# A new written-out order for a one-core attention and feed-forward kernel, with some products moved between two engines

## The chip, the core and the metric

The kernel runs on one core of a Trainium2 chip. The metric is device microseconds of one execution. The kernel before took 254.58 us, the median of three runs (254.56 to 255.01).

## The reference

The computation is linear attention with polynomial sketches, followed by a multiplicative feed-forward block (FFN). In NumPy, cut to what matters:

```python
batch, n_heads, seq, head_dim, r = 4, 4, 1088, 32, 8          # q, k, v: (4, 4, 1088, 32) float32
def phi(x):                                                   # S1, S2: (8, 32) float64
    a = einsum('rd,bhsd->bhsr', S1, x);  b = einsum('rd,bhsd->bhsr', S2, x)
    return einsum('bhsi,bhsj->bhsij', a, b).reshape(..., 64)
q_p, k_p = phi(q), phi(k)
kv  = einsum('bhsf,bhsd->bhfd', k_p, v)
num = einsum('bhsf,bhfd->bhsd', q_p, kv)
den = einsum('bhsf,bhf->bhs', q_p, k_p.sum(axis=2))[..., None] + 1e-06
x = (num / den), laid out as (4 * 1088, 4 * 32)               # 4352 tokens of 128
out = ((x @ w1) * (x @ w2)) @ w3 @ w_out                      # 128 -> 1024 -> 1024 -> 128, float32
```

The sketches and the weights come in as float64 and reach the kernel as raw 64-bit words; it makes float32 of them itself. The denominator is a sum in which much cancels, so the kernel carries it in leading and remaining parts that are multiplied and added apart.

## The kernel before

**Engines and order.** The program is one long list of named steps, some 950 of them, written out by hand in a string `ORDER`. A step issues one or a few instructions on one engine: TensorE (PE), VectorE (DVE), ScalarE (ACT), GpSimd (POOL), or a DMA on the queue of SyncE (SP). The driver runs the list and ties every instruction to the one before it on the same engine, so each engine works through its own steps strictly in the order of the list and waits at a step whose inputs or buffer are not there yet:

```python
    for name in ORDER.split():
        steps.pop(name)()
    for ins in traced[seen:]:
        if ins.engine in last:
            tc.add_manual_dep(ins, last[ins.engine].name, behind, reason="order")
        last[ins.engine] = ins
```

The engine of some steps is chosen by two more lists: `on(name)` gives GpSimd for a name in `POOL`, ScalarE for a name in `ACTS`, VectorE otherwise. A third table, `SLOTS`, says for each kind of buffer which of its buffers the next allocation in the list takes (eight PSUM banks `b`; SBUF kinds `l`, `m`, `s`, `raw`; `x`, three large buffers shared by the loaded keys, values and queries).

**Names of the steps.** The part ahead of the dot says which data, the part behind it what is done.

- `s.*` prepares the sketch matrices: words to float (`words`, `pair`, `low`, `lead`, `sum`, `rest`), transposes (`T`, `tc`), and the tables that later products read (`R`, `blk`, `RC`, `AR`, `KS`, `P`). `c.*` are constants.
- `k0.*` to `k3.*` are the keys of one batch of the four: `load` and `loadr` (main part and remainder of 64 tokens), `max` and `g` (largest value and rounding grid), `lead` (the part on the grid, line 172 to 177) and `rest` (what is left, L596, 1152 elements in each of 128 partitions; `k0` does it in two parts of 512 and 640), `gram0` to `gram4` (L604, the sum over tokens of key times key, 72 products of 32 by 32 or 64 for each batch), then small steps that turn the gram matrix into the split sum for the denominator (`Gm` to `Gb`, `T0` to `Ts`, `N0` to `Nr`; `Nl` and `Nh` for batch 0 alone). `tr`, `kT`, `ab`, `abc` or `abt` sketch the keys, `kp` multiplies the two sketches to 64 features (L622), `kv` and `kvr` multiply them with the values, `kvm`, `kz`, `kvc`, `kqt` and `kq` lay the result out. `kr0` and `kr1` do this for the key remainders of two batches each; `kr*.kp` is a GpSimd product (L785).
- `q0.*` and `q1.*` (`q_part`) are the queries of batch 0 in halves of 512 columns, `q2` and `q3` those of batch 1, `q4` and `q6` batches 2 and 3 whole (`q_wide`), `qr` the remainders of all batches. Their chain is: `tr` (transpose), `max`, `l2`, `l1`, `rm` (split of the query, L954 or L1272), products `A0`, `A1`, `C0`, `C1` on TensorE, their transposes back (`At`, `Ct`, `C0t`, `C1t`), `sm`, `st`, `sh`, `sl`, `sc` (split of the sketched query), `al` (L1097 or L1346), `p01`, `p2`, `p12` (products of the split parts), `dn`, `de`, `rc` (denominator and its reciprocal), `bs` (the second sketch times the reciprocal, L1379), `phi` (the 64 features, L1389 in `q_wide`), `pt` or `pT` (transpose), `x` (product with `kv`), `xT` (the FFN's input). In `q0` the reciprocal is applied behind the product instead (`xs`).
- `w0` and `w1` are halves of w1 and w2, `w2` is w_out, `w3` to `w10` are blocks of 128 rows of w3: `load`, `c` and `m` (top and low words on ScalarE), `j` (shift on VectorE), `a0` and `a1` (integer additions on GpSimd, L442). `f0` to `f7` multiply w3 with w_out once (`t`, `m`, `o`), so the FFN has three products for a token instead of four.
- `g0` to `g7` are the FFN of 512 tokens each, `gr` of the 256 remaining ones. For each of eight chunks `c` of the hidden width: `ca` (L1448) and `cb` (L1458) the two products, `cc` the copy of the first on ScalarE, `cm` their product on VectorE (L1464), `co` the product with the folded weight (L1471; in `gr` the token blocks are apart as `co0` and `co1`, L1478). Then `oT` and `st` (store).
- `warm0` to `warm28` are idle matmuls on TensorE (L221) over a block of zeros, whose result nobody reads: `WARM` gives them 16, 10, 6, 4, 4, 2 (eight times) and 1 (sixteen times) products.

**The work around the change.** The loads and conversions of weights, the four batches of keys and the seven query parts are interleaved with the FFN groups by the list alone. The FFN begins with `g0.3a` and ends with `gr`. The last steps of the list are

```
... gr.2o0 gr.7o0 gr.4o1 gr.oT0 gr.3o1 gr.2o1 gr.7o1 gr.st0 gr.oT1 gr.st1
```

`gr.oT0` is a ScalarE copy out of PSUM, `gr.oT1` one on VectorE; `gr.st0` is issued on ScalarE, `gr.st1` on SP (L1432), each for 128 rows of the output.

Of the kernel before, what the change touches and what calls it, by code (L numbers as in the profile page):

```python
# [41 lines left out]
    "s": "012345671203546710236541073256104",
    "x": "012121021022",
# [9 lines left out]
    k0.Nh k0.rest0 k0.rest1 k1.kp1 k2.kp1 k3.kp0 q0.phi1 q1.al q1.p12 q1.p2 q2.al q2.p12 q2.p2 q2.phi0  # L53
    q3.p2 q4.al q4.p12 q4.phi0 q4.phi1 q6.p12 q6.phi0 q6.phi1 qr.al qr.p2 qr.phi0 s.Pp s.blk s.blkh
    s.low s.rest s.sum
""".split())

ACTS = set("k0.lead1 k1.lead0 k2.lead0 k3.lead0 s.lead".split())
# [39 lines left out]
q6.rm k3.Na q4.xT0 warm6 k3.Nr k3.Nb q4.xT1 g4.2a g2.2o g5.2a g4.2c q6.C0 q6.A0 k3.kvc q6.C1 g5.2c q6.At q6.Ct q6.sm
# [23 lines left out]
def make_steps(ctx, tc, q, k, v, S1, S2, moe_w1, moe_w2, moe_w3, moe_w_out, out):  # L122
# [11 lines left out]
    NT = S // 32  # L134
# [783 lines left out]
    def q_part(key, b, c0, n, kind, xcol=0, xkey=None):  # L918
# [646 lines left out]
```

## Time and profile before

| What the profile of before says | |
| --- | --- |
| time of the profiled execution | 254.37 us |
| its span (first to last instruction) | 252.6 us |
| busy: TensorE products | 246.1 us, 97% of the span |
| busy: TensorE weight loads, beside the products | 137.9 us |
| busy: VectorE | 160.0 us, 358 instructions |
| busy: ScalarE | 99.7 us, 183 instructions |
| busy: GpSimd | 66.8 us, 99 instructions |
| idle matmuls (L221) | 72, busy 13.3 us |
| granted TensorE clock | 1.00 |
| DMA | 22.01 MB, mean 87 GB/s |

How to read it: busy time is that of instructions that compute; issuing a DMA, a register or a semaphore instruction is not counted. Products of TensorE overlap each other, so the sum of their own durations is larger than the busy time. In a row of the timeline stand the start, the busy time, the engine, the line of the kernel, the operation, the output and the inputs by the program's names, the size (partitions x elements) and, in brackets, how long the engine had been idle before and which instruction ended that.

### The profile page before, as it was taken

What the parts mean: (1) busy time and instruction counts of PE and PEld (TensorE: products, weight loads), DVE (VectorE), ACT (ScalarE), POOL (GpSimd) and SP (SyncE); (2) the same over time, 40 slices, a digit from 0 to 9 for tenths busy, and PEclk for the clock granted to TensorE, in tenths of its full rate; (3) what the DMA queues carried; (4) which work ended last, traced back from release to release, by engine and by line L of the source; (5) the groups of instructions that cost most, each with busy time, mean ns of one, the idle gap of its engine ahead of it and who ended that gap; (6) DMA issues with size and microseconds to landing.
All of it is one profiled execution on the core that took longest, in us unless ns stands there. A gap on an engine that the chain in (4) does not pass through costs nothing.

```text
span 252.6 us, 5980 instructions
## 1 busy us (share of the span) xinstructions
PE 246.1 (97%) x2503; PEld 137.9 (55%) x2503; DVE 160.0 (63%) x358; ACT 99.7 (39%) x183; POOL 66.8 (26%) x99
## 2 busy tenths in 40 slices
PE   8799999999999999998999999999999999999994
PEld 6689845457456576456446444444444444456554
DVE  2999998989998995938677597550115371424040
ACT  4588398763918543340225143213340012211010
POOL 4644535393546309203540016010000001000000
PEclk9999999999999999999999999999999999999999
DMA  6867793996679930200000000000000007205014
GB/s 182 262 173 263 222 241 84 259 254 139 160 206 235 249 90 0 85 6 3 3 0 3 3 0 1 4 0 0 3 0 0 0 2 123 44 0 83 0 28 76
DMA packets 31130, 22.01 MB, mean 87 GB/s; under 512 B 21248, under 2 KB 25600, under 8 KB 30976
## 3 DMA queue, kind: packets, MB, share of 16 engines
q1 hardware_dynamic: 30416, 21.05, 33.9%
q10 hardware_dynamic: 688, 0.59, 0.7%
q8 instruction: 19, 0.31, 0.5%
q14 instruction: 7, 0.06, 0.1%
HBM read 19.40 MB, written 2.23 MB: 86 GB/s over the span
## 4 chain that ended last, share of the span: by engine, by line
PE 95%; issue 1%; DMA 1%; POOL 1%; ACT 1%; DVE 0%; SPq 0%; POOLq 0%; ACTq 0%
PE a_ps L1448 23%; PE b_ps L1458 23%; PE ps_o L1471 22%; PE ps_w3o L478 6%; PE ps_g L604 3%; PE ps_x L1408 2%; PE idle_ps L221 2%; PE ps_ac L1294 2%; PE ps_kv L714 2%; PE ps_or L1478 1%; DMA s_raw<-in_S_dram 1%; PE ps_ab L672 1%; PE ps_ab L647 1%; PE ps_xt L1195 1%; PE ps_kt L630 1%
## 5 line engine op out<-in xcount | busy, mean ns | idle before, releaser
L1464 DVE TENSOR_TENSOR ab<-ffa,b_ps 128x512 f32<-128x512 f32 (+1 forms) x72 | 44.9, 649 | 60.8 <-PE b_ps L1458 40.9
L1453 ACT COPY ffa<-a_ps 128x512 f32<-128x512 f32 (+1 forms) x72 | 38.6, 566 | 96.4 <-PE a_ps L1448 93.8
L1448 PE MATMUL a_ps<-xT,w 128*128 128x512 f32 (+1 forms) x144 | 66.7, 570 | 0.0
L1458 PE MATMUL b_ps<-xT,w 128*128 128x512 f32 (+1 forms) x144 | 65.5, 569 | 0.0
L1471 PE MATMUL ps_o<-ab,w3o 128*128 128x512 f32 x128 | 62.3, 594 | 0.0
L1448 PEld LDWEIGHTS a_ps<-xT,w 128*128 128x128 f32 x144 | 26.5, 190 | 30.0 <-issue 23.9
L1458 PEld LDWEIGHTS b_ps<-xT,w 128*128 128x128 f32 x144 | 26.9, 190 | 29.1 <-issue 25.0
L1471 PEld LDWEIGHTS ps_o<-ab,w3o 128*128 128x128 f32 x128 | 23.9, 190 | 25.5 <-issue 24.0
L442 POOL TENSOR_TENSOR w3c<-cv_c,cv_m 128x512 int32<-128x512 int32 x16 | 20.8, 1333 | 22.0 <-DVE cv_c L431 13.7
L1389 POOL TENSOR_TENSOR ph<-s_al,s_bs 128x1024 f32<-128x1024 f32 (+1 forms) x6 | 10.8, 1808 | 52.7 <-DVE s_bs L1379 52.7
L478 PEld LDWEIGHTS ps_w3o<-wo,w3T 128*128 128x128 f32 x128 | 15.4, 192 | 3.6 <-issue 3.3
L478 PE MATMUL ps_w3o<-wo,w3T 128*128 128x128 f32 x128 | 15.6, 275 | 0.0
L221 PE MATMUL idle_ps<-zeros 128*128 128x256 bf16 x72 | 13.3, 317 | 1.0 <-DVE zeros L193 1.0
L229 ACT ACTIVATE cv_c<-raw 128x1024 f32<-128x1024 f32 x11 | 12.8, 1175 | 2.1 <-DMA raw<-in_moe_w_dram 2.1
L417 ACT ACTIVATE cv_m<-raw 128x1024 int32<-128x1024 uint32 x11 | 12.8, 1178 | 0.0
L472 DVE STREAM_TRANSPOSE w3T<-w3c 128x1024 f32<-128x1024 f32 x8 | 9.8, 1230 | 3.5 <-POOL w3c L442 3.5
L604 PE MATMUL ps_g<-kk 128*32 128x64 f32 x288 | 8.2, 225 | 2.1 <-POOL kk L596 1.1
L1346 POOL TENSOR_TENSOR s_al<-s_hl 128x128 f32<-128x128 f32 (+2 forms) x3 | 2.3, 753 | 29.7 <-DVE s_hl L1341 29.7
L1419 ACT COPY xT<-ps_x 128x128 f32<-128x128 f32 (+2 forms) x20 | 4.6, 325 | 13.1 <-PE ps_x L1408 9.5
L1397 DVE STREAM_TRANSPOSE pT<-ph 128x1024 f32<-128x1024 f32 (+1 forms) x7 | 8.2, 1164 | 2.5 <-POOL ph L1389 2.4
L221 PEld LDWEIGHTS <-zeros 128*128 128x128 bf16 x72 | 7.5, 114 | 3.9 <-issue 1.0
L604 PEld LDWEIGHTS ps_g<-kk 128*32 128x32 f32 x288 | 7.0, 109 | 2.8 <-POOL kk L596 1.2
(241 smaller groups left out, 284.3 us busy)
## 6 DMA issues: line engine op xcount, KB each, us to landing
raw<-in_moe_w_dram SPq DMA_DIRECT2D x32, 256.0 KB, 7.6
qh<-in_q_dram SPq DMA_DIRECT2D x4, 544.0 KB, 3.5
out_dram<-oT SPq DMA_DIRECT2D x33, 64.0 KB, 2.0
raw<-in_moe_w_dram SPq DMA_DIRECT2D x4, 512.0 KB, 5.8
k<-in_k_dram SPq DMA_DIRECT2D x3, 512.0 KB, 5.9
v<-in_v_dram SPq DMA_DIRECT2D x2, 512.0 KB, 6.4
raw<-in_moe_w_out_dram SPq DMA_DIRECT2D x1, 1024.0 KB, 6.0
kh<-in_k_dram SPq DMA_DIRECT2D x8, 128.0 KB, 6.3
```

What stands on the lines that cost most here:

```text
L221: pe.matmul(t, zeros, bview(zeros, [[0, 2], [1, 128]]), start=True, stop=True)
L229: act.activation(dst, hi.bitcast(F32), ACT.Prelu, scale=2.0 ** -112, alpha=-2.0 ** 32)
L417: act.mul(x["m"], words(0).bitcast(U32), 2.0 ** -29)
L442: pool.tensor_tensor(d, c, m, ALU.add)
L478: pe.matmul(t["o"], w3T[ko][:, c], wo[:, c], start=c == 0, stop=c == NC - 1)
L604: pe.matmul(o[h * D:(h + 1) * D], lhs, rhs, start=start, stop=stop, skip_group_check=True)
L1389: on(nm(f"phi{u}")).tensor_mul(x, bview(s["al"][:, u * g], [[r, g], [1, r], [0, r]]), bview(s["bs"][:, u * g], [[r, g], [0, r], [1, r]]))
L1448: pe.matmul(x["a"][:, :w], w_of(0, c), xT[g][:, c0:c0 + w], start=True, stop=True)
L1453: act.copy(x["s"][:, :w], x["a"][:, :w])
L1458: pe.matmul(x["b"][:, :w], w_of(1, c), xT[g][:, c0:c0 + w], start=True, stop=True)
L1464: dve.tensor_mul(ab_sb[g, c][:, c0:c0 + w], x["s"][:, :w], x["b"][:, :w])
L1471: pe.matmul(o_ps[g], w3o[:, c], ab_sb[g, c], start=c == 0, stop=c == NC - 1)
```

## The change

The order of all steps is new, and with it `SLOTS`. The steps are the same but for the last store, and so are `WARM` and the products on TensorE. Three things are not order:

- **Engines.** From VectorE to GpSimd go `k0.Nl k1.kp0 k2.rest0 k3.kp1 q0.al q0.p01 q1.p01 q2.p01 q3.p01 q3.p12 q3.phi0 q3.sc q4.bs q4.sc q6.al q6.bs q6.sc qr.p01 qr.sc`, from GpSimd to VectorE `k1.kp1 q1.al q1.p12 q2.p12 q2.p2 q4.p12 q4.phi0 q6.p12 q6.phi0 q6.phi1 qr.al qr.phi0 s.sum`, and from ScalarE to VectorE `s.lead` and `k3.lead0`.
- **Choice.** `rm`, `sc`, `p01` and `bs` get their engine by `on(name)` now.
- **The last store.** `gr.st1` writes the first 64 of its 128 rows and stays on SP; a new `gr.st2` writes the other 64 and is issued on ScalarE's queue. The list now ends with all `o1` products ahead of the last `o0` ones.

```diff
 QUARTERS = (0, 2, 1, 3)
 POOL = set("""
-    k0.Nh k0.rest0 k0.rest1 k1.kp1 k2.kp1 k3.kp0 q0.phi1 q1.al q1.p12 q1.p2 q2.al q2.p12 q2.p2 q2.phi0
-    q3.p2 q4.al q4.p12 q4.phi0 q4.phi1 q6.p12 q6.phi0 q6.phi1 qr.al qr.p2 qr.phi0 s.Pp s.blk s.blkh
-    s.low s.rest s.sum
+    k0.Nh k0.Nl k0.rest0 k0.rest1 k1.kp0 k2.kp1 k2.rest0 k3.kp0 k3.kp1 q0.al q0.p01 q0.phi1 q1.p01 q1.p2
+    q2.al q2.p01 q2.phi0 q3.p01 q3.p12 q3.p2 q3.phi0 q3.sc q4.al q4.bs q4.phi1 q4.sc q6.al q6.bs q6.sc
+    qr.p01 qr.p2 qr.sc s.Pp s.blk s.blkh s.low s.rest
 """.split())
-ACTS = set("k0.lead1 k1.lead0 k2.lead0 k3.lead0 s.lead".split())
+ACTS = set("k0.lead1 k1.lead0 k2.lead0".split())
 ORDER = """
-s.load k1.zero c.ident c.mask k0.zero c.zeros warm0 k0.loadr k0.load0 k0.load1 c.act s.words s.pair s.lead q0.load
-k0.max0 k0.max1 k0.g k0.lead0 warm1 k1.loadr s.low s.sum s.four k0.tr0 k0.lead1 s.rest s.T k0.kT0 k0.rest0 warm8 q0.tr
-q1.tr q1.max q0.max warm3 k1.load kr0.load s.P k0.gram0 k0.gram1 s.Pc s.tc k0.rest1 warm14 kr0.tr s.R k0.gram2
-k0.gram3 q0.l2 s.c k0.gram4 k0.tr1 s.Pm k1.max q0.restT s.blk k0.Gm q0.l1 k0.Gt s.Pp s.zero k0.kT1 k0.ab0 kr0.kT
-k0.abc0 k0.Ga v0.zero s.blkh k0.ab1 k0.T0 k0.Gb q0.rm k0.T1 warm26 k1.g k0.kp0 k0.Ta k0.Tb k0.abc1 warm2 k0.Ts k0.kp1
-k1.lead0 k1.tr1 warm23 q0.A0 warm15 w1.load kr0.ab warm4 warm12 kr0.abc k1.rest0 q1.l2 warm13 warm7 warm18 q0.C0 k0.N0
-kr0.kp w1.m v0.load q0.sma q0.C0t q0.sta k0.N1 k0.kv0 k0.kv3 k1.gram0 k1.gram1 k0.kv1 q1.l1 k0.kv2 kr1.load v0.loadr
-k0.kvr s.RC k0.Na warm10 warm21 kr1.tr k0.kvc k0.kvm q0.sha q0.sla k0.Nb k2.zero k0.Nh w0.load warm17 k1.tr0 kr1.kT
-q0.sca k1.kT1 k1.kT0 k0.kzt q1.A0 k0.kz q0.A1 kr1.ab q0.al q0.phi0 q0.phi1 q1.sm q0.smy q0.sty q1.st q0.pt0 warm5
-k0.kqt k0.Nl warm20 k0.Nf w0.m kr1.abc q0.pc0 q0.pt1 q0.shy q1.rm q0.C1 k1.gram2 k1.gram3 k1.gram4 q0.pc1 warm19 q0.x0
-q1.load k0.Nr q0.sly q0.C1t q0.x1 w0.c q0.scy q0.p01 q0.p2 q1.sh q0.p12 q0.dn s.KS w0.j q1.C0 q0.de q1.sl q0.rc q0.xs
-q0.xt q0.xT k1.ab w0.a1 v1.zero k2.load k2.loadr k2.max w1.c warm24 w0.a0 warm22 g0.3a q1.sca q1.p01 g0.3c k2.g
-v1.loadr k1.Gm k2.lead0 q1.scy q1.al w2.load q1.p2 q1.p12 k1.abt q1.restT q1.dn g0.1a g0.3b w1.j q1.de k0.kq q1.rc
-k1.Gt g0.3m q1.bs g0.2b w1.a0 q1.phi g0.0a g0.5a g0.4a q1.pt0 g0.0c w2.c g0.1c w3.load w2.m k2.rest0 q1.pt1 g0.6a
-g0.2a q1.pc0 w2.j k1.Ga k1.kp0 q1.pc1 g0.5c g0.2c g0.6c k2.gram0 q2.tr k1.Gb k1.T0 k2.gram1 k1.T1 q2.max k1.Ta k1.Tb
-k1.Ts w2.a0 w4.load q1.x w1.a1 k2.gram2 k2.gram3 k2.gram4 k1.N0 k1.N1 s.AR warm16 k2.Gm q1.xT g1.7a q2.l2 k2.Gt k2.Ga
-g0.6b g0.0b w3.c q2.l1 k1.Na k1.Nb k1.Nr k2.Gb w4.m g0.4c g0.6m g0.1b g0.7a g0.0m q2.rm w4.c q2.C0 q2.A0 q2.C1 g0.1m
-w4.j w3.j g1.7c warm28 g0.7c w3.m g1.4a g1.2a g0.7b q3.tr q2.Ct g0.2m g1.6a q2.At g1.6c w4.a0 w3.a0 g1.1a g1.7b
...
-gr.5o0 gr.1o0 gr.4o0 gr.0o1 g4.oT gr.6o1 gr.5o1 gr.3o0 g6.oT g4.st g6.st gr.1o1 gr.2o0 gr.7o0 gr.4o1 gr.oT0 gr.3o1
-gr.2o1 gr.7o1 gr.st0 gr.oT1 gr.st1
+c.zeros s.zero k0.zero c.mask c.ident s.four k0.load1 k0.load0 s.load c.act warm17 warm16 warm5 warm0 warm26 k1.zero
+k0.tr0 k0.tr1 s.words s.pair s.low s.lead s.sum s.rest k0.loadr k0.max0 q0.load warm3 k0.max1 warm28 s.T k0.g k0.lead0
+q0.tr s.P k0.kT0 s.tc s.R k1.load k0.lead1 q1.tr k0.rest0 k0.rest1 q0.max warm1 k1.loadr k1.max k1.tr0 q0.restT s.c
+q0.l2 q0.l1 s.Pc k0.kT1 w1.load k1.g k0.gram0 k0.gram1 k0.gram2 k0.gram3 k0.gram4 s.Pm q1.max s.blk k0.Gm s.blkh
+k0.ab0 k0.Gt warm24 k0.Ga k0.Gb k1.lead0 k0.T0 k0.T1 warm27 s.KS q0.rm warm2 k0.Ta v0.zero k0.ab1 warm11 k0.abc0 q0.A0
+k0.Tb s.Pp k1.rest0 v0.load v0.loadr k0.Ts warm4 warm9 k0.N0 k0.N1 q0.C0 k0.kp0 k0.Na k0.abc1 warm7 warm14 kr0.load
+kr0.tr q0.sma kr1.load k0.Nb k0.kp1 q0.sta k0.Nh k2.zero warm10 k1.tr1 w1.m w1.c kr0.kT kr0.ab q0.A1 q1.l2 k0.Nf k0.Nl
+q0.sha q1.l1 k0.kv0 kr0.abc k1.kT0 w0.load kr0.kp k1.gram0 k0.kv3 k1.kT1 k0.kv1 q0.C1 k0.kv2 q0.sla k0.kvr q0.C0t
+q1.load q0.sca q0.al q0.C1t q0.phi0 q0.smy q0.sty warm13 k0.kvm q1.A0 warm15 k0.Nr q0.shy warm22 kr1.tr warm6 warm8
+warm23 warm12 k0.kzt k0.kz k0.kvc q0.sly q0.phi1 q1.sm q0.scy q1.rm q1.st q0.p01 q0.p2 q0.pt0 warm20 k1.gram1 k1.gram2
+k1.gram3 k1.gram4 k2.load k2.loadr w0.c q0.pt1 w0.j q0.p12 q1.sh q0.dn s.AR q0.de q0.pc0 q0.x0 q0.rc w1.j q0.pc1 q0.x1
+q0.xs q1.C0 q0.xt q1.sl w1.a0 w0.m k1.ab k2.max k0.kqt w0.a0 k1.Gm k1.Gt q1.scy q0.xT q1.sca k1.Ga g0.4a q3.tr g0.5a
+kr1.kT q1.p01 q1.al k1.abt q1.p2 k2.g s.RC v1.zero q1.p12 w1.a1 k0.kq g0.3a v1.loadr k2.lead0 w0.a1 g0.6a q1.restT
+g0.2a g0.5b q1.dn q2.tr q1.de q1.rc q1.bs w3.load g0.2c g0.3c w3.c g0.3b g0.2b k1.Gb q1.phi q1.pt0 g0.6c g0.5c g0.0a
+q1.pt1 k1.T0 q1.pc0 k1.T1 g0.3m q2.max q2.l2 q1.pc1 g0.5m k1.Ta k1.Tb w6.load w4.load k1.Ts k2.rest0 k2.gram0 k2.gram1
+k2.gram2 k2.gram3 k2.gram4 q1.x w3.m k1.N0 k1.N1 q2.l1 k1.kp1 k1.Na q2.rm k1.Nb g0.4b g0.7a q3.max k2.Gm w2.load g0.4c
+q1.xT k1.kp0 g0.0c g0.7c k1.Nr g0.2m k2.Gt w3.j g1.5a g1.7a w3.a0 g1.5c w3.a1 v1.load k2.Ga g0.4m q2.C0 q2.A0 q2.C1
+q2.At q2.Ct k3.zero g1.7b q2.sm q2.st q2.sh q2.sl q2.sc q2.p01 q2.al g1.2a g1.0a g0.0b g1.4b w6.m w6.c w4.c q3.l2
+k2.Gb q3.l1 g1.7c g1.7m g0.0m g1.1a q2.p2 g0.1a kr1.ab g0.6b g1.0c w2.m w2.c g0.1c g1.1c kr1.abc q2.p12 q2.dn q2.de
+g1.2c w4.m w4.j q2.rc q3.rm q2.load w9.load w4.a0 w4.a1 k2.T0 k1.kv0 k2.T1 k2.Ta q2.bs k1.kv2 k1.kv3 k1.kv1 k1.kvr
+q3.C0 k1.kvc w2.j g0.6m q3.A0 q3.C1 q3.Ct w8.load g1.1b w2.a1 q2.phi0 g0.1b k1.kqt k1.kq g1.1m q3.At f1.t f0.t g1.4a
+g1.5b q2.restT g1.5m k2.Tb q2.pT0 g1.3b g1.3a g1.0b g1.6a w2.a0 g1.3c g1.4c w9.m g1.6c w9.c w6.j g1.3m g1.4m k2.Ts
+q3.sm g0.1m q3.st f1.m k2.N0 k2.N1 q2.x0 k2.Na v3.zero w6.a0 k2.Nb w6.a1 w8.c q2.xT0 q3.sh w5.load q4.tr f0.m g1.6b
+w8.m q3.sl w8.j w8.a0 q3.sc g2.6a g2.4a g2.2a g2.0a g2.6c f0.o f3.t g2.0c g2.5a g2.1a g2.5c w5.c g2.1c g1.0m g1.6m
...
+k2.kT1 g0.5o f4.m k3.g g2.0m f4.o g2.4m k2.kT0 q4.At q4.Ct f7.t k3.lead0 g3.2a g1.0o g2.7b f7.m f7.o g2.7m k3.rest0
+g3.4a g3.4c q4.sm q4.st g3.5a q4.sh g3.6a k3.gram0 k3.gram1 kh3.load q3.load k3.gram2 g3.2c q3.restT g3.5c k3.gram3
+k3.gram4 k2.ab qr.max q4.sl q4.sc v2.zero q4.p01 warm21 g0.4o k2.abt k3.Gm k3.Gt g3.5b g2.0o g2.4o g1.1o g2.5b k3.Ga
+g3.5m k3.kT1 g1.2b q4.al g1.2m q6.tr q4.p2 g1.6o k3.Gb k3.kT0 k2.kp0 kr1.kp q6.max warm19 g1.3o g1.4o v2.load v2.loadr
+g3.1a g1.5o g3.0a qr.l2 g2.5m g3.0c q6.l2 g3.6c g3.6b q4.p12 k2.kp1 q4.dn g3.6m g2.6o g2.1b k3.ab g3.1c v3.load
...
+gr.3c g0.st g6.1c gr.1a g6.4b gr.4b gr.2b g7.st g6.1m gr.6m g6.4m g4.oT gr.1c gr.4a g6.2o g6.6o gr.7b gr.1b gr.7m
+gr.1m gr.3b g6.4o g6.1o g6.3o gr.4c gr.0o1 g6.7o gr.6o1 g1.st gr.5o1 gr.0o0 gr.1o1 gr.6o0 g4.st g2.st gr.5o0 gr.2m
+gr.4m gr.3m g6.oT gr.4o1 g6.st gr.3o1 gr.2o1 gr.1o0 gr.7o1 gr.4o0 gr.3o0 gr.2o0 gr.7o0 gr.oT0 gr.oT1 gr.st2 gr.st1
+gr.st0 warm25
 """
...
-            dve.scalar_tensor_tensor(s["q2"], s["q1"], 2.0 ** 16, s["qT"], ALU.mult, ALU.add)
+            on(nm("rm")).scalar_tensor_tensor(s["q2"], s["q1"], 2.0 ** 16, s["qT"], ALU.mult, ALU.add)
...
-                    dve.tensor_add(s["lo" + x], s["lo" + x], s[C])
+                    on(nm("sc" + x)).tensor_add(s["lo" + x], s["lo" + x], s[C])
...
-            dve.tensor_mul(s["pr"][:, :2], s["hla"], bview(s["hiy"], [[0, 2], [1, W]]))
+            on(nm("p01")).tensor_mul(s["pr"][:, :2], s["hla"], bview(s["hiy"], [[0, 2], [1, W]]))
...
-            dve.tensor_add(by16(s["lo"]), by16(s["lo"]), s["Cx"])
+            on(nm("sc")).tensor_add(by16(s["lo"]), by16(s["lo"]), s["Cx"])
...
-            dve.tensor_mul(s["bs"], s["Cb"], bview(s["rc"], [[1, G], [0, r]]))
+            on(nm("bs")).tensor_mul(s["bs"], s["Cb"], bview(s["rc"], [[1, G], [0, r]]))
...
-    def rest_dst(oT, u):
-        (sp if u else act).dma_start(bass.AP(tensor=out.tensor, offset=(NT - 2 + u) * DM,
-                             ap=[[NT * DM, 32], [S * DM, B], [1, DM]]), oT)
+    def rest_dst(oT, u, t0=0, n=32):
+        (sp if u and not t0 else act).dma_start(bass.AP(tensor=out.tensor, offset=(NT - 2 + u + t0 * NT) * DM,
+                             ap=[[NT * DM, n], [S * DM, B], [1, DM]]), oT[t0 * B:(t0 + n) * B])
...
-                step(f"g{g}.st{u}")(lambda u=u: dst(z[u], u))
+                if u == 0:
+                    step(f"g{g}.st0")(lambda: dst(z[0], 0))
+                else:
+                    for i in range(2):
+                        step(f"g{g}.st{1 + i}")(lambda i=i: dst(z[1], 1, 16 * i, 16))
```

## The prediction, made before the changed kernel ran

> **What bounds the kernel now.** I read the page first, then the table of stretches, the waits of TensorE, the groups by form on GpSimd, and the timeline at four places.
>
> ```profile
> PE 246.1 (97%) x2503; PEld 137.9 (55%) x2503; DVE 160.0 (63%) x358; ACT 99.7 (39%) x183; POOL 66.8 (26%) x99
> ...
> L221 PE MATMUL idle_ps<-zeros 128*128 128x256 bf16 x72 | 13.3, 317 | 1.0 <-DVE zeros L193 1.0
> ```
> ```profile
> 0.00:9.29 9.29, 7.01 (x46) 5.02 (x46) 4.30 (x12) 4.92 (x11) 4.77 (x37) 1.00 0.77 221
> 9.29:30.29 21.00, 21.00 (x578) 18.97 (x578) 20.11 (x61) 14.28 (x30) 10.66 (x19) 1.00 0.68 219
> 30.29:70.00 39.71, 39.68 (x499) 21.42 (x498) 36.75 (x94) 29.59 (x43) 20.96 (x20) 1.00 0.80 192
> ...
> 110.00:150.00 40.00, 39.01 (x538) 19.82 (x538) 26.38 (x57) 14.22 (x26) 8.61 (x7) 1.00 0.01 2
> ...
> 200.00:249.41 49.41, 49.41 (x217) 26.90 (x215) 17.52 (x33) 7.58 (x20) 1.07 (x1) 1.00 0.27 42
> ```
> ```profile
> PE ps_g L604 <- POOL kk L596: 1.1, 1, 1.1
> PE idle_ps L221 <- DVE zeros L193: 1.0, 1, 1.0
> PE ps_g L604 <- issue: 1.0, 1, 1.0
> ```
>
> The columns of the table are length, then busy time of PE, PEld, DVE, ACT and POOL. TensorE is full from 9.29 us (first `k0.gram0`) to its end at 249.41; VectorE is nearly full to 70. The only later wait of TensorE is 1.0 us of "issue". So an order can win only in four places: the time of the first FFN product (30.29 us, `a_ps`), idle matmuls that stand among real ones, that pause, and the tail of 3.17 us (249.41 to 252.58). The profiled run took 254.37, 1.79 beyond its span; the median is 254.58, 0.21 more. I work in the span and add 2.0.
>
> **Idle matmuls.** The old order has ten behind the first FFN product (`warm16`, `28`, `27`, `25` one each, `11`, `9`, `6` two each); the new one has three (`warm21`, `19`, `18`), and `warm25` behind the last product. TensorE starts one each 0.11 to 0.12 us in the trace and did not wait around them: 7 x 0.115 = **-0.8**. All other products stay, same shapes, so TensorE has 219.1 - 0.8 = 218.3 us between first FFN product and end, pause included.
>
> **Front.** VectorE sets it: from 5.63 us on it stops almost never. I sum start-to-start times of its steps ahead of `q0.xs` (28.01). Leaving: `q0.al` 0.33, `k0.Nl` 0.10, `q0.p01` 0.34 (to GpSimd), `q1.sl` 0.34 (to behind) = 1.1. Coming: `w1.j` 0.60, `s.AR` 0.20, `s.lead` 0.36 (from ScalarE), `s.sum` 0.17 = 1.3; the last two fall into the 0.87 us in which VectorE waits for `k0.loadr` before 5.63. Net -0.3. Against it: `q0.phi0` now waits for `q0.al` on GpSimd (0.46 to 0.70 by its 128x128 rows, 0.30 of it covered by `q0.C1t`): +0.2 to +0.4. `k0.lead1` stands behind `s.tc` on ScalarE, which needs TensorE; it slips some 0.3, `k0.rest1` with it, and `k0.Gm` moves to about 12.35 from 12.09, as `k1.max`, `k1.g` and `q1.max` are ahead of it anyway. On SP's queue `kr0.load` goes behind `v0.load`, whose buffer is now that of `q0`, so it is issued near 12.5 instead of 4.25; with 4.5 us to landing it is there at 17, and `kr0.tr` is now behind `q0.C0` near 18. Without that cover each microsecond delays `k0.kvr`, `k0.kz` and `q0.x0`. TensorE has 36 idle matmuls and eight more transposes ahead of `k0.gram0`, then 32 to the FFN, against 32 and 30: cover for waits. I take **0**, bounds -0.3 and +0.8; the upper is `kr0.kp` ahead of `q0.al` on GpSimd at 1.78 us instead of 0.63:
>
> ```profile
> 17.38 1.36 DVE L596 TENSOR_TENSOR kk<-k,kk 128x1152 f32<-128x1152 f32 x1
> 17.45 1.78 POOL L785 TENSOR_TENSOR kpr<-krab 128x256 f32<-128x256 f32 x1 [3.57 <-DVE kp L622]
> ...
> 61.00 0.95 DVE L1272 SCALAR_TENSOR_TENSOR q<-q,qT 128x512 f32<-128x512 bf16 x1
> ...
> 101.91 0.63 POOL L785 TENSOR_TENSOR kpr<-krab 128x256 f32<-128x256 f32 x1
> ```
>
> The same product takes 0.63 alone and 1.78 beside a VectorE step with two SBUF inputs; at 61.00 it was VectorE that lost 0.27 to a running `q2.al`.
>
> **Moved products.** Over the kernel VectorE loses about 2 us and GpSimd gains 6. Where buffers and engines leave TensorE slack it costs nothing; it counts at the narrowest place. `k2.rest0` (1152 elements) goes from VectorE (1.35) to GpSimd; rows of 512 and 640 elements there took 1275 and 1555 ns, so 2.2 ns an element and 2.7 us. From `q0.xs` at 28.0 VectorE has 4.9 us to the end of `k2.g` (with `k2.max` 1.26, `q3.tr` 0.63, `k1.abt` 0.70 in it); `k2.lead0` on ScalarE 2.55; so `k2.rest0` can start near 35.4, or behind `q1.phi` (1.2, two SBUF inputs, VectorE reaches it at 35.1 to 35.6) near 36.7, and ends at 39.4. TensorE asks for it (`k2.gram0`) after nine pairs of 0.86, eight transposes and two small products, 9.2 us after 30.3: 39.5. Nothing to spare. Next, `f1.m` needs `w2.a0`, now behind `w4.a0`, `w4.a1`, `w2.a1` and `q2.phi0` on GpSimd: 3 x 1.28 + 1.95 + 1.3 to 2.0 = 7.1 to 7.8 us from the end of `w4.m`, 0 to 0.9 late by my sums. Later stages have a microsecond or more: `q3.pT0`, `q4.C0` and `k3.gram0` come ready 1.5 to 3 us ahead. A delay of TensorE is paid once, as it gives all others room: **+0.6**, bounds 0 and 1.5.
>
> **The pause.** It stands inside 248 short products in a row:
>
> ```profile
> q8 instruction: 1, 0.02, 1.9%
> ```
> ```profile
> 117.22 0.27 PE L604 MATMUL ps_g<-k,kk 128*32 128x32 f32 x4
> 118.47 0.22 PE L604 MATMUL ps_g<-kk 128*32 128x64 f32 x1 [0.99 <-issue]
> ```
>
> One 16 KB packet of the instruction queue falls in 115.5 to 118.6 (it began at 116.15), and 19 such packets stand against 5006 matmuls and weight loads, so one serves some 256 instructions, or 128 products. Short ones pass at 12 ns; 128 take 1.5 us, less than the 2.3 from 116.15 to 118.47. In the new order `k3.gram` and `k2.ab` make 160 in a row. Counting instructions to there, a boundary falls within a few of `k3.gram0`, so it should recur: old 1.2, new 1.0 (bounds 0 and 1.2): **-0.2**. [...] The trace shows a pause, and I follow it.
>
> **Tail.** Old: last product, `gr.oT1` 0.29, `gr.st1` issued on SP.
>
> ```profile
> 248.85 0.64 ACTq L1432 DMA_DIRECT2D out_dram<-oT  x1
> ...
> 249.45 0.29 DVE L1498 COPY oT<-ps_or 128x128 f32<-128x128 f32 x1 [2.85 <-PE ps_or L1478]
> 249.77 0.62 SPq L1432 DMA_DIRECT2D out_dram<-oT  x1
> ```
>
> New: the `o1` products end four products earlier, so `gr.st1` is early; but ScalarE does `gr.oT0` (0.27) after the last product, then issues `gr.st2`, then `gr.st0`. The last issue starts one issue later: 0.3 (shortest of SP's rows) to 0.64 (its own row); half the rows, I take **+0.5**.
>
> **Sum.** -0.8 + 0 + 0.6 - 0.2 + 0.5 = +0.1: span 252.7, time 254.7. What a measurement can tell is about 0.2%, 0.5 us.
>
> **Rivals.** (a) As summed, 254.0 to 255.7: chance 0.45. (b) Faster: pause gone and arrivals in time: 0.1 - 1.0 - 0.6 = -1.5, 253.1; for it, a boundary a few instructions earlier falls among 0.43 us products; against it, the places with nothing to spare. 0.25. (c) Slower: `k2.rest0` gets to GpSimd before `q1.phi` gets to VectorE. Then `q1.phi` starts at 38.1, ends at 39.3, and `q1.pt0` waits from 37.4 to 39.4: 2.0 instead of 0.6, 256.1; with the 0.8 of the front, 257. It decides when `k2.lead0` ends before `q1.bs`. For it: GpSimd work beside two-input steps everywhere; against: `w0.a1` still holds GpSimd near 35.5. [...] 0.25. (d) The store in halves does what its name says and ends earlier by half an issue (-0.3), with VectorE's lighter queue giving another 0.3 in front: -1.0 against the sum, 253.7. 0.05.
>
> Faster: (b), (d) and little of (a): 0.30. Within 0.2%: more than half of (a): 0.26. Slower: (c) and the upper part of (a): 0.44. Range: 252.9 to 257.2; (a) alone 254.0 to 255.7.
>
> **What would show it.** First `a_ps` at 30.0 to 31.1; idle before `ps_g` near 39.5 or before `ps_ph` near 37.4 (c); an "issue" wait near 108 in `ps_g`; the last ACT issue 0.9 us after the last product. A first `a_ps` before 29.5, or waits of TensorE after 30 us over 3 us in sum, would make the prediction wrong.

## The result, and the profile after

The changed kernel takes 266.16 us (median of four executions, 263.4 to 267.81) against 254.8 for the one before: a ratio of 1.041, 95% interval 1.033 to 1.049. Ratios, here and below, are of means and leave out an execution that counts as slow, over 1.5% above the fastest of its kernel; here that of 267.81. The kernel is slower by some 11 us where no change to speak of was forecast (254.7, range 252.9 to 257.2). Its profiled execution took 263.40, with a span of 261.6; that is the one read here.

The head of the page of after. The first digits of a row stand for slices of 6.5 us.

```profile
span 261.6 us, 5978 instructions
PE 249.5 (95%) x2503; PEld 140.1 (54%) x2503; DVE 169.3 (65%) x355; ACT 95.7 (37%) x177; POOL 72.3 (28%) x105
...
PE   8999946999999999999999999999999999999992
...
PEclk9999995899999999999999999999999999999997
```

TensorE has a hole in the sixth slice, and the granted clock is 0.50 from 40.32 to 47.15, in the seventh and eighth. The table of stretches (length, busy time of PE, PEld, DVE, ACT and POOL, granted clock, DMA share, GB/s), cut at the first FFN product (30.62), at that hole, at `k2.gram0` (47.96) and at the last product's end (256.65), and the waits of TensorE:

```profile
9.82:30.62 20.80, 20.40 (x569) 18.14 (x568) 19.76 (x59) 14.99 (x26) 10.08 (x16) 1.00 0.68 190
...
35.93:41.20 5.27, 0.00 (x1) 0.03 (x1) 5.17 (x5) 2.64 (x5) 4.48 (x2) 0.92 1.07 229
41.20:47.96 6.76, 6.75 (x18) 3.33 (x19) 3.19 (x5) 1.30 (x3) 0.00 (x0) 0.56 0.15 33
47.96:110.00 62.04, 62.04 (x809) 36.44 (x807) 54.81 (x117) 37.14 (x62) 31.93 (x28) 1.00 0.61 156
...
256.65:261.60 4.95, 0.11 (x2) 0.00 (x0) 0.00 (x0) 0.27 (x1) 0.00 (x0) 0.71 0.17 39
```
```profile
PE b_ps L1458 <- DVE G_b L810: 5.3, 1, 5.3
PE idle_ps L221 <- DVE zeros L193: 1.0, 1, 1.0
PE ps_ac L1294 <- issue: 0.6, 1, 0.6
PE ps_g L604 <- POOL kk L596: 0.4, 1, 0.4
```

The span grew by 9.0 us in three places. The first FFN product comes 0.33 later (30.62 against 30.29). From there to the last product's end it takes 226.03 instead of 219.12, 6.91 more. Behind that end it takes 4.93 (to the end of the span at 261.58) instead of 3.17, 1.76 more. In the middle part there is one wait of 5.3 us: `g0.3b` wants the PSUM bank of batch 1's gram matrix, which `k1.Gb` on VectorE frees. Why VectorE is late shows the timeline of VectorE and GpSimd:

```profile
33.63 0.69 DVE L1253 STREAM_TRANSPOSE qT<-qh 128x512 f32<-128x512 f32 x1
34.25 6.20 DVE L1121 SCALAR_TENSOR_TENSOR s_rc<-s_d 128x16 f32<-128x16 f32 x1
40.48 0.25 DVE L1125 RECIPROCAL s_rc<-s_rc 128x16 f32<-128x16 f32 x1
```
```profile
33.42 2.51 POOL L445 TENSOR_TENSOR w<-w,cv_m 128x512 int32<-128x512 int32 x2
35.90 2.61 POOL L596 TENSOR_TENSOR kk<-k,kk 128x1152 f32<-128x1152 f32 x1
38.48 1.93 POOL L622 TENSOR_TENSOR kp<-kabt 128x1024 f32<-128x1024 f32 x1
```

The same step in before, and behind it `w1.a0` on GpSimd:

```profile
33.35 0.17 DVE L1121 SCALAR_TENSOR_TENSOR s_rc<-s_d 128x16 f32<-128x16 f32 x1
33.51 1.28 POOL L445 TENSOR_TENSOR w<-w,cv_m 128x512 int32<-128x512 int32 x1 [1.13 <-DVE s_rc L1121]
```

`q1.de` adds two sums of 16 numbers a partition. In the trace of before it took 0.17 us; here it takes 6.20 and ends when GpSimd's row `w1.a1`, `w0.a1`, `k2.rest0`, `k1.kp0` does. The four have no gap between them, and the last two stand there by the change. Behind `q1.de`, in VectorE's order, come `q1.rc`, `q1.bs`, `k1.Gb` and `q1.phi`.

### The profile page after: what moved, and what is told of

Its sections match the earlier page's. It is cut to its first block, busy times and chain, and to the rows that moved or that the text cites. A ratio compares the mean times of both kernels' runs of the same rounds, so it can differ in the third digit from the quotient of the medians.

```text
span 261.6 us, 5978 instructions
## 1 busy us (share of the span) xinstructions
PE 249.5 (95%) x2503; PEld 140.1 (54%) x2503; DVE 169.3 (65%) x355; ACT 95.7 (37%) x177; POOL 72.3 (28%) x105
## 4 chain that ended last, share of the span: by engine, by line
PE 82%; DVE 13%; DMA 2%; issue 1%; SPq 0%; POOL 0%; ACT 0%; DVEq 0%; ACTq 0%
PE b_ps L1458 23%; PE ps_o L1471 21%; PE a_ps L1448 21%; PE ps_w3o L478 6%; DVE s_rc L1121 2%; PE ps_ac L1294 2%; PE ps_x L1408 2%; DMA k<-in_k_dram 2%; DVE k_m L180 2%; PE ps_or L1478 1%; PE ps_g L604 1%; PE ps_kv L714 1%; DVE kp L622 1%; DVE kk L596 1%; PE ps_ph L1173 0%
## 5 line engine op out<-in xcount | busy, mean ns | idle before, releaser
L1453 ACT COPY ffa<-a_ps 128x512 f32<-128x512 f32 (+1 forms) x72 | 37.8, 567 | 98.2 <-PE a_ps L1448 92.2
L1458 PE MATMUL b_ps<-xT,w 128*128 128x512 f32 (+1 forms) x144 | 68.5, 586 | 5.3 <-DVE G_b L810 5.3
L1448 PE MATMUL a_ps<-xT,w 128*128 128x512 f32 (+1 forms) x144 | 65.1, 575 | 0.0
L1471 PE MATMUL ps_o<-ab,w3o 128*128 128x512 f32 x128 | 60.5, 594 | 0.0
L442 POOL TENSOR_TENSOR w3c<-cv_c,cv_m 128x512 int32<-128x512 int32 x16 | 21.6, 1374 | 27.5 <-DVE G_a L170 14.4
L1341 POOL TENSOR_TENSOR s_hl<-s_hl,ay_C 128x512 f32<-128x512 f32 (+2 forms) x4 | 3.7, 929 | 57.8 <-DVE s_hl L1337 57.8
L221 PE MATMUL idle_ps<-zeros 128*128 128x256 bf16 x72 | 12.7, 316 | 1.0 <-DVE zeros L193 1.0
L1487 DVE STREAM_TRANSPOSE oT<-ps_o 128x512 f32<-128x512 f32 x8 | 5.7, 708 | 6.6 <-PE ps_o L1471 6.6
L482 ACT COPY w3o<-ps_w3o 128x128 f32<-128x128 f32 x8 | 2.0, 268 | 15.7 <-PE ps_w3o L478 15.7
```

The source lines that it names most:

```text
L221: pe.matmul(t, zeros, bview(zeros, [[0, 2], [1, 128]]), start=True, stop=True)
L442: pool.tensor_tensor(d, c, m, ALU.add)
L1448: pe.matmul(x["a"][:, :w], w_of(0, c), xT[g][:, c0:c0 + w], start=True, stop=True)
L1453: act.copy(x["s"][:, :w], x["a"][:, :w])
L1458: pe.matmul(x["b"][:, :w], w_of(1, c), xT[g][:, c0:c0 + w], start=True, stop=True)
L1471: pe.matmul(o_ps[g], w3o[:, c], ab_sb[g, c], start=c == 0, stop=c == NC - 1)
```

## The experiments

Three theories stood at the start. P: a VectorE step with two SBUF inputs cannot run while GpSimd works through a row without a gap (that a port is the reason was my guess; no run shows it). A: an accident of one execution. B: `q1.de` waited for something of its own. The kernel before, run beside the first four experiments, took 254.4 (253.69 to 255.01); beside the later ones it took 254.3 to 254.7.

**The changed kernel again.**

> The changed kernel once more, unchanged. Theory P (port): q1.de, a VectorE step with two SBUF inputs, cannot run while GpSimd works through instructions without a gap; its 6.20 us in the trace of after should come again (5.5 to 6.5), with a wait of TensorE of 5 to 6 us for k1.Gb near 36 and a granted clock near 0.5 behind it for some 7 us; time 263 to 268. Rival A (accident): the 6.20 us was one execution's disturbance; q1.de takes under 0.5 us and the time is near 255.

Measured: 266.73 (264.7 to 267.57), ratio 1.048. `q1.de` again takes 6.20 us (39.83 to 46.03), so it is no accident. The low clock (0.50) behind the wait lasts 3.4 us here, though, not the 6.8 of after. The execution differs in one more place: TensorE waits 4.2 us for "issue" near 20 us.

```profile
PE b_ps L1458 <- DVE G_b L810: 4.6, 1, 4.6
PE ps_g L604 <- issue: 4.2, 1, 4.2
```

**Both moved steps back.**

```diff
-    k0.Nh k0.Nl k0.rest0 k0.rest1 k1.kp0 k2.kp1 k2.rest0 k3.kp0 ...
+    k0.Nh k0.Nl k0.rest0 k0.rest1 k2.kp1 k3.kp0 ...
```

> After, with k2.rest0 and k1.kp0 back on VectorE. Theory P: GpSimd's row of instructions without a gap now ends with w0.a1 at about 35.9, so q1.de ends near 36.0 instead of 40.4 (1.7 us instead of 6.2); TensorE waits some 1 us for k1.Gb instead of 5.3, the low clock behind the wait is gone (3.4 us); VectorE has 1.35 and 1.2 us more to do ahead of k2.gram0 and later, which may give back up to 1.5. Time 255.5 to 257.5. Rival B (q1.de waited for something of its own, a semaphore or its input): q1.de still takes about 6 us and the time stays over 262.

Measured: 259.31, ratio 1.021 (1.0175 to 1.0244), over the 255.5 to 257.5 expected. `q1.de` takes 1.71 us and ends with `w0.a1`; TensorE waits 0.8 us for `k1.Gb`. B falls.

```profile
33.16 2.50 POOL L445 TENSOR_TENSOR w<-w,cv_m 128x512 int32<-128x512 int32 x2
33.99 1.71 DVE L1121 SCALAR_TENSOR_TENSOR s_rc<-s_d 128x16 f32<-128x16 f32 x1
```

But `k2.rest0` on VectorE now stands behind `k1.Ts`, ends at 42.97, and TensorE waits 2.7 us for it at `k2.gram0`: the price of the step at that place of VectorE's order, which I had put at up to 1.5.

**A gap in GpSimd's row, behind `q1.rc`.** Engines as in after.

```diff
             dve.reciprocal(s["rc"], s["rc"])
+            if key == 1:
+                t = consts.tile([128, 1], F32, tag="rc_seen")
+                pool.tensor_copy(t, s["rc"][:, :1])
```

> After, with one GpSimd copy of a single column added that reads the result of q1.rc and stands between w0.a1 and k2.rest0; engines are as in after. Theory P: GpSimd waits for q1.rc, so q1.de gets its turn at 35.9 when w0.a1 ends, and ends near 36.0. Then k2.rest0 and k1.kp0 start at about 36.3 and follow one another without a gap to 40.8, and now q1.phi, which also has two SBUF inputs and comes at about 36.9, is held to 40.8 and ends at 42.0, and TensorE waits about 1 us for k1.Gb and 3 to 4 us at q1.pt0. Time 259 to 264. Rival B: q1.de keeps its 6 us. Rival C (one instruction at a time: VectorE gets in between two GpSimd instructions): q1.phi starts when k2.rest0 ends, at 38.9.

Measured: 257.51, ratio 1.012 (1.0094 to 1.0145), under the 259 to 264 expected. `q1.de` takes 1.71 us again, with both steps still on GpSimd: what counts for it is whether they follow without a gap, not that they are there. `q1.phi` was held as expected, but less long than a whole row:

```profile
36.58 2.63 POOL L596 TENSOR_TENSOR kk<-k,kk 128x1152 f32<-128x1152 f32 x1
36.94 3.35 DVE L1138 TENSOR_TENSOR ph<-s_al,s_bs 128x1024 f32<-128x1024 f32 x1
39.17 2.94 POOL L622 TENSOR_TENSOR kp<-kabt 128x1024 f32<-128x1024 f32 x1
```

It was held for 2.1 us until `k2.rest0` ended, got in there, and `k1.kp0` took 2.94 instead of 1.93. So P in its strict form (the whole row) holds for `q1.de` and not for `q1.phi`, which went as C said.

**The gap behind `q1.phi`.**

```diff
                 phi("phi", 0, nj, s["bs"])
+                t = consts.tile([128, 1], F32, tag="ph_seen")
+                pool.tensor_copy(t, s["ph"][:, 0, 0, 0, :1])
```

> After, with one GpSimd copy of a single column added that reads the result of q1.phi and stands between w0.a1 and k2.rest0; engines are as in after. Theory P: q1.de is held by w1.a1 and w0.a1 alone (to 35.9), q1.phi runs free (36.8 to 38.1), and k2.rest0 follows at 38.2 to 40.8. TensorE waits about 1 us for k1.Gb and under 1 us at k2.gram0; no low clock. Time 255 to 257, the new order's gain of 0.8 in idle matmuls and its loss of 1.8 behind the last product included. Rival B: q1.de keeps its 6 us and the time stays over 262.

Measured: 256.5, ratio 1.0064 (1.0036 to 1.0092), one copy of one column against 1.041. Four of its five executions took 255.56 to 256.51, the fifth, of which there is no trace, 261.48. `q1.phi` runs free (36.37, 1.22 us). Of the waits of TensorE behind 30 us there are left 0.9 us for `k1.Gb`, 0.2 for `k2.rest0` and a pause of 0.9 under "issue" near 140.

**One step of the row back.**

```diff
-    k0.Nh k0.Nl k0.rest0 k0.rest1 k1.kp0 k2.kp1 k2.rest0 k3.kp0 ...
+    k0.Nh k0.Nl k0.rest0 k0.rest1 k2.kp1 k2.rest0 k3.kp0 ...
```

> After, with k1.kp0 back on VectorE, so the row of GpSimd instructions without a gap is w1.a1, w0.a1 and k2.rest0. Theory P (the whole row holds q1.de): q1.de ends when k2.rest0 ends, 4.2 us after its start instead of 6.2; TensorE waits 3.3 us instead of 5.3, and the low clock is shorter or gone. Time 257 to 261. Rival C (at each end of a GpSimd instruction VectorE may win): q1.de ends 0.4 or 1.7 us after its start. Rival B: no change of q1.de.

Measured: 260.62, ratio 1.0229 (1.021 to 1.0248).

```profile
34.11 4.28 DVE L1121 SCALAR_TENSOR_TENSOR s_rc<-s_d 128x16 f32<-128x16 f32 x1
...
35.74 2.62 POOL L596 TENSOR_TENSOR kk<-k,kk 128x1152 f32<-128x1152 f32 x1
```

4.28 us, to the end of the row once more, which is now that of `k2.rest0`. TensorE waits 2.7 us for `k1.Gb`, with 3.4 us of low clock (0.50) behind it.

**Work for TensorE in the hole.** 46 idle matmuls ahead of `g0.5b`'s product.

```diff
                     x["b"] = ps("h", [128, 512], "b_ps")
+                    if (g, c) == (0, 5):
+                        for _ in range(46):
+                            pe.matmul(x["b"][:, :256], zeros, bview(zeros, [[0, 2], [1, 128]]), start=True, stop=True)
```

> After, with 46 idle matmuls added in g0.5b, just ahead of its product and into its bank, so that TensorE has some 5.3 us of work in the time in which it waited for k1.Gb (46 x 0.115). Theory T (throttle): the low clock behind the wait (0.54 and 0.61 of full speed from 40 to 48 us in after) comes from the 5.2 us of idle TensorE alone; with idle matmuls in it the granted clock stays at 1.00, q1.de still takes about 6.2 us, and the time falls by some 3.4, to 260 to 261, in executions without another pause. Rival (the low clock comes from something else in this stretch, such as the DMA load of 1.05 of the engines' time there): the clock still falls to near 0.5 and the time stays where it was or grows.

Measured: 260.92, ratio 1.0232 (1.0208 to 1.0256). `q1.de` is held as in after (it alone keeps VectorE busy from 36 to 40 us), and the clock stays at 1.00:

```profile
36.10:41.40 5.30, 4.90 (x40) 3.70 (x38) 5.20 (x5) 2.70 (x5) 4.50 (x3) 1.00 1.04 225
41.40:45.21 3.81, 3.81 (x18) 2.11 (x19) 3.09 (x5) 1.29 (x3) 0.00 (x0) 1.00 0.05 13
```

From `g0.3b` to `k2.gram0` the same work takes 3.81 us at a clock of 1.00, and 6.76 at 0.56 in after. So what brings the low clock there is the idle time of TensorE (5.27 us in after, 0.4 here) and not the DMA load (a share of 1.07 in after, 1.04 here), and it costs 2.95 us. The whole profiled execution gains less, 1.8 us (261.64 against 263.40), as it loses 1.0 again behind `k2.gram0`, 0.7 of it in a pause under "issue".

**Three tests of why `q1.de` loses at every end of a GpSimd instruction, where `q1.phi` got in at one.** First `q1.de` 24 times as long, then as the operation of `q1.phi`, then in front of the transpose:

```diff
-            dve.scalar_tensor_tensor(s["rc"], s["d"][:, 1], EPS, s["d"][:, 0], ALU.add, ALU.add)
+                s["dw"] = bview(s["pr"], [[24, 16], [1, 24]])
+                dve.scalar_tensor_tensor(s["dw"], bview(s["d"][:, 1], [[1, 16], [0, 24]]), EPS,
+                                         bview(s["d"][:, 0], [[1, 16], [0, 24]]), ALU.add, ALU.add)
```

> After, with q1.de writing each of its 16 sums 24 times (384 elements a partition instead of 16), and q1.rc reading every 24th; nothing else. It asks why q1.phi with 1024 elements got in at the next end of a GpSimd instruction (39.2 in the run with a gap behind w0.a1) while q1.de with 16 lost at three such ends. Theory L (length decides): the longer q1.de gets in at the first end of a GpSimd instruction, so it takes about 0.4 + 0.5 us, and w0.a1, which follows, takes longer by as much; TensorE does not wait for k1.Gb. Rival O (the instruction that stands ahead of it, or the GpSimd operations, decide): it is held to the end of the row again, 6.2 us or more.

```diff
-            dve.scalar_tensor_tensor(s["rc"], s["d"][:, 1], EPS, s["d"][:, 0], ALU.add, ALU.add)
+                dve.tensor_add(s["rc"], s["d"][:, 1], s["d"][:, 0])
```

> After, with q1.de as a plain addition of the two sums (its small constant 1e-06 is left out in this query part), that is the operation of q1.phi (tensor_tensor) instead of scalar_tensor_tensor; same size, same place. Theory O2 (the operation decides who gets in at the end of a GpSimd instruction): q1.de ends 0.4 us after its start. Rival (size or place decides): it is held 6.2 us again.

```diff
-... q1.dn q2.tr q1.de ...
+... q1.dn q1.de q2.tr ...
```

> After, with q1.de ahead of the transpose q2.tr in VectorE's order instead of behind it (q1.dn q1.de q2.tr); nothing else. q1.de then comes to VectorE at 33.7, 0.3 us into w1.a1 on GpSimd. Theory (the step ahead decides: a transpose that has only just ended makes VectorE late at the first end of a GpSimd instruction): q1.de gets in at 34.7 and TensorE does not wait. Rival (short steps lose at every such end): it is held to 40.4, 6.7 us, and q2.tr with it, and the time is that of after.

Measured: held for the whole row each time (262.5 to 263.3 us in the profiled executions; the first variant ran four times, from 262.51 to 269.57, the others once): 6.57 us with 384 elements, 6.18 as a plain addition, 6.71 in front of the transpose.

```profile
33.67 6.71 DVE L1121 SCALAR_TENSOR_TENSOR s_rc<-s_d 128x16 f32<-128x16 f32 x1
```

Then the other way round, the run with the gap behind `q1.rc`, with `q1.phi` in four parts:

```diff
-                phi("phi", 0, nj, s["bs"])
+                for j in range(nj):
+                    phi("phi", j, 1, s["bs"])
```

> The run with a copy behind q1.rc (k2.rest0 and k1.kp0 back to back beside q1.phi) with q1.phi cut into four products of 256 elements instead of one of 1024; nothing else. Theory L (a short VectorE step loses at the end of a GpSimd instruction when another follows, a long one gets in): the first part is held until k1.kp0 has ended, near 41.1, TensorE waits 3 us or more at q1.pt0, and the time grows by about 1.5 over the run with the whole q1.phi. Rival N (the place decides: at this end VectorE gets in): the first part ends near 39.5, as the whole one got in at 39.2.

Measured: 262.47 in its one execution, which had a pause of 2.8 us under "issue" near 20 us and so can't be set against the 257.51 of the whole `q1.phi`. TensorE's rows for `q1.pt0` show that the first part of 256 elements got in when `k2.rest0` ended (42.48), and the other three were held until `k1.kp0` ended at 44.57:

```profile
42.91 0.30 PE L1177 MATMUL ps_ph<-ident,ph 128*128 128x128 f32 x1 [0.83 <-DVE ph L1138]
...
44.90 1.00 PE L1177 MATMUL ps_ph<-ident,ph 128*128 128x128 f32 x3 [1.70 <-DVE ph L1138]
```

So neither length (16, 384; 256, 1024), nor operation, nor the step ahead decides. What does is open; what is shown is the two bounds, one GpSimd instruction and the whole row.

**One move alone, in the old order.**

```diff
-    s.low s.rest s.sum
+    s.low s.rest s.sum k2.rest0
```

> Before, with k2.rest0 on GpSimd: one move of the change alone, in the old order. There q1.de (33.35) ran ahead of w1.a0 (33.51), so no row of GpSimd instructions holds it. Theory P: k2.rest0 meets w1.a0's end at 34.8 and q1.phi, which waits there. If q1.phi gets in first, k2.rest0 runs 35.9 to 38.5, k1.kp0 (two SBUF inputs on VectorE) is held to 38.5 and k1.Gb and k1.T0 behind it come about 1 us later: 0 to +1 us. If k2.rest0 gets in first, q1.phi is held to 37.4 and TensorE waits 1.5 to 2 us at q1.pt0: +1.5 to +2.6. Rival M (the move itself is what costs, wherever it stands): a step of VectorE is held for over 5 us and the time grows by over 5.

Measured: 255.39 against 254.72, ratio 1.0033 (1.0005 to 1.0062). The move costs 0.3% there: `q1.phi` starts first (34.77), `k2.rest0` takes 3.67 us, TensorE waits 0.8 us for `k1.Gb`. Rival M falls. What I had not expected: `w2.j`, which has one SBUF input, was held too (2.44 us against 0.69).

```profile
34.77 1.22 DVE L1135 TENSOR_TENSOR ph<-s_al,s_bs 128x1024 f32<-128x1024 f32 x1
34.84 3.67 POOL L596 TENSOR_TENSOR kk<-k,kk 128x1152 f32<-128x1152 f32 x1
36.62 2.44 DVE L431 TENSOR_SCALAR wo<-cv_c 128x1024 int32<-128x1024 int32 x1 [0.63 <-ACT cv_c L229]
```

**The last store as before,** with the gap behind `q1.phi`.

```diff
-gr.4o0 gr.3o0 gr.2o0 gr.7o0 gr.oT0 gr.oT1 gr.st2 gr.st1
+gr.4o0 gr.3o0 gr.2o0 gr.7o0 gr.oT0 gr.oT1 gr.st1
 gr.st0 warm25
...
+                step(f"g{g}.st{u}")(lambda u=u: dst(z[u], u))
```

> After, with the one-column GpSimd copy that reads q1.phi ahead of k2.rest0, and with the last store as before: gr.st1 writes all 128 rows on SP, no gr.st2. Theory S: in after gr.st1 was issued at 258.72 because it waited for the landing of gr.st2 (2.6 us on SP), so the time behind the last product is 4.95 us against 3.17 in before; with one store gr.st0 is the last one issued, about 0.3 us after gr.oT0, and the end comes about 3.2 to 3.5 us after the last product: 1.4 to 1.8 less than the run with the copy alone, 254.2 to 255.0. Rival: the tail is set by ScalarE's issue (gr.st0 behind gr.oT0) and gains under 0.5.

Measured: 255.0, ratio 1.0005 (0.9992 to 1.0018). Behind the last product it takes 3.32 us, against 4.92 in the run with the gap alone: 1.6 us for the halves. In after SP's queue shows the wait, and the timeline the issue (column: start, length):

```profile
SPq L1432 <- DMA out_dram<-oT: 2.6, 1, 2.6
```
```profile
256.69 0.27 ACT L1498 COPY oT<-ps_or 128x128 f32<-128x128 f32 x1 [9.64 <-PE ps_or L1478]
256.75 1.32 ACTq L1432 DMA_DIRECT2D out_dram<-oT  x2
258.72 0.62 SPq L1432 DMA_DIRECT2D out_dram<-oT  x1
```

`gr.oT1` was ready at 256.09, but `gr.st1` was issued at 258.72, right when `gr.st2` had landed (258.65): the halves run one after the other, across two queues. Why `gr.st1` waits for that landing is open. With its two faults mended the new order is as fast as the old one, no more. In this execution the first FFN product is 0.66 later (30.95), the middle 0.23 shorter and the tail 0.15 longer; in the middle, fewer idle matmuls (0.8) and a pause that is down from 1.0 to 0.2 stand against waits of 0.7 for `k1.Gb` and 0.2 for `k2.rest0`. Nine of its ten executions took 254.33 to 255.42, the tenth, of which there is no trace, 259.92.

**The idle matmuls.** The kernel before without its ten behind the first FFN product.

```diff
-        warm(f"warm{i}", n)
+        warm(f"warm{i}", 0 if i in (6, 9, 11, 16, 25, 27, 28) else n)
```

> Before, without its ten idle matmuls behind the first FFN product (warm6, 9, 11, 16, 25, 27, 28); nothing else. Theory I (the prediction's first term): each costs 0.115 us of TensorE, which waits for nothing around them, so the time falls by 10 x 0.115 = 1.15, to 0.9955 of before (0.994 to 0.998). Rival: TensorE only arrives earlier at what it waits for (the pause near 117, k2.gram0, the transposes of the query parts), and the time stays within 0.2%.

Measured: 253.06 against 254.72, ratio 0.9924 (0.9896 to 0.9951): faster than both kernels, and by more than the theory gave (0.994 to 0.998). In its trace 1.17 us of this lies behind the first FFN product, as expected; but the pause of 1.0 near 117 is gone as well, with a wait of 0.3 for VectorE in its place, so not all of the 1.17 need be the matmuls. The first product was 0.33 earlier in this execution.

**Why executions of the changed kernel differ by 4 us.** Two more of it:

> The changed kernel once more. Theory F (fetch): an execution near 263 has no pause of TensorE for instructions ahead of 30 us; one near 266 to 268 has one of about 4 us there, with a granted clock near 0.5 behind it. Rival: the difference lies elsewhere (the length of the low clock behind the wait for k1.Gb, the tail).

> The changed kernel once more; expectations as for the run before it: near 263 without a pause for instructions ahead of 30 us, near 266 to 268 with one of about 4 us.

Measured: 261.84 and 262.24, both without a pause between 20 and 30 us (TensorE busy 10.00 of 10.00). With the two traces above that makes three of 261.8 to 263.4 without and one of 266.7 with (4.2 us, 19.85 to 24.03, the clock at 0.50 for 6.8 us from 22.3 on). The run with `q1.phi` in four parts had one too (19.85 to 22.62). The views put both under "issue"; that instructions came late was my theory, and what brings the pause is open. Whether the other executions above 266 had it is not known, as they have no trace.

## Why the prediction was wrong, step by step

**The step that failed** is the one on moved products, "late arrivals", taken at +0.6 with bounds 0 and 1.5. It measured 5.27 of waiting and 2.95 of low clock, 8.2 us. Three faults in it:

- I followed `k2.rest0` into `q1.phi` only, and let the steps between (`q1.de` above all) run at the length of their rows in before. But `q1.de` reads two SBUF tiles as well and reaches VectorE at 34.25, when `w1.a1` and `w0.a1` already run. In the trace of before it ran (33.35) ahead of `w1.a0` (33.51), so its row of 0.17 us was one without a neighbour.
- The hold was priced as one instruction, and `k1.kp0` in the row was not looked at. `k2.lead0` ended at 35.63, before `w0.a1` did (35.93), so `k2.rest0` followed without a gap, and `k1.kp0`, whose input `k1.abt` was ready at 33.0, followed that. The length of the row is the price, 6.2 us. Rival (c) had the hold and its condition right (`k2.lead0` ends before `q1.bs`), chance 0.25, but the wrong step, and 1.4 us over the sum where this term came out 7.6 over it (8.2 instead of 0.6).
- I had no price for what TensorE's idle time does to its clock. The trace of before could not show it: its longest wait in the middle is 1.0 us.

The sign that I had named came: after 30 us TensorE waited for 5.9 us, not under 3.

The traces show `q1.de` held over two, three and four GpSimd instructions (1.71, 4.28 and 6.20 us), for up to 6.71 us. They show the hold and what ends it, not its cause.

**The other terms.** Idle matmuls, -0.8: it fits the run without them and what is left of the 6.91 (5.27 + 2.95 - 0.8 - 0.4 = 7.0), though neither measures it alone. Front, 0 with bounds -0.3 and +0.8: it measured +0.33, and +0.03 and +0.10 in two more executions; `kr0.kp` ran alone in 0.65. Pause, -0.2: it measured -0.4, but that it came near is luck. It did not come at `k3.gram`, where I had counted a packet's end with 256 instructions for each (5006 over 19 packets is 263), but in the short products of `q6.C1` at 147 with 0.6 (0 to 0.6 in the four traces of the changed kernel). Later places (`f1.m`, `q3.pT0`, `q4.C0`): no wait, as argued, though with 8 us more of room than I had reckoned with. Tail, +0.5: it measured +1.76. The last ACT issue came 0.84 us behind the last product, as forecast, but I had called `gr.st1` early and not asked whether it waits for its other half; in before `gr.st0` and `gr.st1` do not wait for each other (issued at 248.85 and 249.77).

Rival (b), arrivals in time and no pause, was not reached even with the faults mended (ratio 1.0005). Rival (d) fell: the halves were not faster but 1.6 us slower.

## What to carry to other kernels

Before moving a step to GpSimd, write down GpSimd's whole row without a gap around it, and look for VectorE steps behind its start, however small: `q1.de`, with two SBUF inputs, was held to the end of the row (6.20 us instead of 0.17), and everything behind it in VectorE's order with it; `w2.j`, with one, took 2.44 us instead of 0.69. If such a row can't be avoided, a gap of one tiny instruction that waits for VectorE's last urgent step was enough here (1.041 became 1.006). The TensorE wait of 5.3 us had a second price of 2.95 us in the clock behind it, and idle matmuls inside the wait saved that (1.8 us of it was left in the whole execution). Without ten that covered none the kernel before was 0.8% faster, though not all of that is shown to be theirs.

## What the runs showed of the hardware that was not expected

- A VectorE instruction of 16 elements a partition (384 in one run) was held by four GpSimd instructions in a row: 6.20 us in after and in its first repeat, 6.57 with 384 elements, 6.18 as a plain addition, 6.71 in front of the transpose. Rows of three and two held it for 4.28 and 1.71 us. A longer one (1024 elements, 3.35 us instead of 1.22), and the first of four short ones (256), got in at an end between the same two GpSimd instructions.
- The granted clock fell to 0.50 behind waits of TensorE: in after at 40.32, 4.4 us after the last product ahead of the wait, in the first repeat 2.5 us and in the run with one step back 3.3 us after it. It stayed there for about 6.8 us (five waits of 4.2 to 5.7 us; 6.83 in after) or about 3.4 us (waits of 2.7, 2.8 and, in the first repeat of the changed kernel, 4.6 us). Another wait of 2.7 us, in the run with both steps back, left it at 1.00. So the length of a wait alone does not give its price, and the 2.95 us of after is not fixed; what decides is open.
- TensorE paused in the front in two executions, with no releaser that the views show ("issue"): for 4.2 us from 19.85 on, with the clock at 0.50 for 6.8 us from 22.3 on, and for 2.8 us from 19.85 on, with 0.50 for 3.4 us from 23.1 on. In after and in its two later repeats TensorE was busy for 9.96, 10.00 and 10.00 of the 10 us from 20 to 30.
